# The first microseconds of a fused MLP kernel: x's first block turned by half-height products, its loads and the biases moved

## The chip, the cores and the metric

The kernel runs on one core of one Trainium2 chip. The metric is the device time of one execution in microseconds (us). Three runs of the kernel before gave a median of 265.3 us (264.82 to 265.36). TensorE is called PE here (its weight loads PEld), VectorE DVE, ScalarE ACT, GpSimd POOL, and SyncE, which only issues transfers, SP.

## The reference

The kernel computes a dense layer with a tanh-approximated GELU and a second dense layer, and all gradients, in bf16:

```python
B, S, D, F = 1, 2048, 448, 1792
h   = gelu(x @ w1 + b1)          # x: S x D, w1: D x F
out = h @ w2 + b2                # w2: F x D
# outputs: out, and from grad_out the gradients of x, w1, b1, w2, b2
```

## The kernel before, in words

The sequence is cut into four blocks of 512 rows. Within a block the 14 tiles of 128 columns of F are taken in seven pairs, so 28 pairs in all. For pair p, `u{p}` is x @ w1 (before GELU), `q{p}` is grad_out @ w2 turned; ACT and DVE make h and its derivative from u (steps `c`, `s`, `g`, `t` and `e`, `r`, `y`, `z`, `m`, `n`, `G`), and out and the gradient of x are summed from them on PE (`p`, `o`, `x`). After the four blocks, two stretches of full-height products (lines L781 and L835) make the gradients of w1 and w2.

Nothing is scheduled by a tool: four strings, `PE_ORDER`, `ACT_ORDER`, `DVE_ORDER` and `SP_ORDER`, list the steps of each engine in order, and each engine takes its own strictly in that order. The places of all buffers are fixed by name; the waits between engines follow from who reads and writes which buffer. A wait for a PSUM bank follows the tile: `bank0` to `bank5` are six tiles of one bank, but banks 6 and 7 are the two halves of one tile, `qb`.

In blocks 0 to 3 the contraction over D = 448 and over pairs is done by half-height products: the array's rows 0 to 63 and rows 64 to 127 hold different weights and write to two different banks at once (`run`, line L241). A run has a direction d = 1 or 2, in which the halves change banks; before the second direction a word from POOL's sequencer (line L236) tells PE that the first has ended.

The start, which the change touches:

- `xr01`, `xr12`, `xr24` load rows of x's first block (tiles of 128 rows: 0; 1; 2 and 3) into `TR`. `L0` to `L4` load w1's columns in five parts (into `w1f`), `Z0` to `Z2` the last rows of w1 for block 0 (into `gh_nat`), `K0` to `K3` load w2, `b1` and `b2` the biases. `X1`, `Y0`, `J..` and `I..` are loads that turn on the way.
- PE warms up with `W6` (six products of ones over 512 columns). `X0` to `X3` turn the four tiles of x by products with an identity matrix, which DVE makes at the start (`ident`, lines L560 to L569), four products of 128 columns each, full height, tile t into bank t. `w4` is four more products of ones, over 128 columns.
- The turned tiles are copied from PSUM into `xT`: X0 and X2 on DVE, X1 and X3 on ACT (line L583).
- Pair 0 of u is made in halves of 256 columns: `h0.1` and `h0.2` (the two directions, banks 4 and 5) need only X0 and X1; `h1.1` and `h1.2` (banks 2 and 3) need X2 and X3. Then `u1.1` and on.
- `B` spreads b2 over all partitions by a product with ones into bank 6, and `b2c` (L705, DVE) copies it to `b2_bc`. b1 is turned by four DVE transposes (`b1T`, L676); every evacuation of u (`c`, lines L411 on ACT and L413 on DVE) adds b1 from there.
- POOL clears three small tiles at the start, the buffer behind b2 among them (`b2z`, L672).

Of the kernel before, what the change touches and what calls it, by code (L numbers as in the profile page):

```python
# [127 lines left out]
SP_ORDER = """  # L128
xr01 xr24 b1 L1 Z1 L2 L3 K0 L4 K1 Z2 K2 K3 X1 R F Y0 J0 J1 J2 Y1 I0 E J3 I1 So0.1 So0.0 X2 H0 H1 H2 H3 H4 H5 H6 H7 H8 H9
T0 T1 H10 T2 H11 T3 H12 T4 H13 T5 So1.0 So1.1 T6 T7 H14 T8 Y2 H15 T9 X3 H16 T10 H17 Sx0.0 Sx0.1 T11 H18 H19 T12 H20  # L130
# [30 lines left out]
def make_plan(tc, ctx, x, w1, b1, w2, b2, grad_out, out_0, out_1, out_2, out_3, out_4, out_5):  # L161
    nc = tc.nc
    P = 128
# [63 lines left out]
    def run(slots, idle=False):  # L227


        first = slots[0]  # L230
        prev = [tail_of.get((first[i][0], 1 - i), (0, None, False)) for i in (0, 1)]
        prev = max([t for i, t in enumerate(prev) if t[2] or not first[i][4]], default=(0, None), key=lambda t: t[0])
        n_run[0] += 1
        word = None
        if prev[0] > seen[0]:
            word = nc.gpsimd.nop()  # L236
            tc.add_manual_dep(word.ins, prev[1].ins.name, DEP, reason="the run has ended")
            seen[0] = prev[0]
        for two in slots:
            for i, (b, n, l, r, st, sp) in enumerate(two):  # L240
                m = nc.tensor.matmul(bk_(b)[:, 0:n], lhsT=l, rhs=r, start=st, stop=sp, skip_group_check=True)  # L241
# [122 lines left out]
    def wake(n, w=SB):  # L364
# [3 lines left out]
        pe("wake", fn, [], [bank(("wake", len(pl.lists["PE"])), 7)], ("wake", n), (None, 0))  # L368

    def OP(p, i):  # L370
        c = p % NPB
        UN("o", p // NPB, 1 - i % 2, [2 * c, 2 * c + 1], 1 + i // 2)
# [16 lines left out]
    for p in range(NPAIR):  # L389
        val(("ub", p), F_UB[p])  # L390
        val(("h", p), ("hT", (p // NPB) % 2, p % NPB))
        val(("gh", p), ("ghT", (p // NPB) % 2, p % NPB))
        if p == NTR - 1:
            val(("xrows", 0), ("TR0", p))
            val(("xrows", 1), ("TR1", p))
# [85 lines left out]
    stage_of = {}  # L481
    val("b2z", ("stage", NST - 1))
    val("b2r", ("b2r",))
    val("ident", ("stage", 0))
# [68 lines left out]
    def LXN(t0, t1, eng="SP"):  # L553

        src = x2[t0 * P:t1 * P, :].rearrange("(t p) d -> p t d", p=P)
        dma(eng, f"xrows{t0}", x_rows[:, t0:t1, 0:D], src, [], [("xrows", t // 2) for t in range(t0, t1)], (t1 - t0) * 114688)

    def identity():
# [10 lines left out]
        nc.vector.tensor_scalar(out=ident, in0=nums128, scalar1=row, scalar2=None, op0=ALU.is_equal)  # L569

    def XT(t):

        def fn():
            for k in range(4):
                c = min(k * P, D - P)
                nc.tensor.matmul(bk_(t)[:, k * P:(k + 1) * P], lhsT=x_rows[:, t, c:c + P], rhs=ident,  # L576
                                 start=True, stop=True, skip_group_check=True)
        pe(f"xt{t}", fn, [("xrows", t // 2), "ident"], [bank(("xt", t), t)], ("s128", 4), (None, 0))

    def XC(t, eng):  # L580
        out = xT[0][:, :, EDGE + t * P:EDGE + (t + 1) * P]
        src = bk_(t)[:, :].rearrange("p (k s) -> p k s", k=4)
        fn = (lambda: nc.scalar.copy(out=out, in_=src)) if eng == "ACT" else (lambda: nc.vector.tensor_copy(out=out, in_=src))  # L583
        pl.op(eng, f"xc{t}", fn, [("xt", t)], [val(("xT", 0, t // 2), ("xT", 0, t // 2))], ("copy", 512))

# [58 lines left out]
    for t in PE_ORDER.split():  # L644
# [5 lines left out]
        elif k == "X":  # L650
            XT(int(a))
        elif k == "B":
            pe("b2u", lambda: nc.tensor.matmul(bk_(6)[:, 0:D], lhsT=one[0:64, 0:P], rhs=stage[NST - 1][0:64, 0, :], start=True, stop=True,  # L653
                                               skip_group_check=True), ["b2r", "b2z"], [bank(("b2u",), 6)], ("s448", 1), (None, 0))
        elif k == "d":
# [15 lines left out]
    pl.op("POOL", "b1z", lambda: nc.gpsimd.memset(b1n[:], 0.0), [], ["b1z"], ("tiny", 1))  # L671
    pl.op("POOL", "b2z", lambda: nc.gpsimd.memset(stage[NST - 1][0:64, 0, :], 0.0), [], ["b2z"], ("tiny", 1))  # L672

    def b1_turn():
        for i in range(4):
            nc.vector.transpose(out=b1T[32 * i:32 * i + 32, :], in_=b1n[:, 32 * i:32 * i + 32])  # L676

    step = {"g": G_, "s": S_, "t": T_, "e": E_, "r": R_, "y": Y_, "z": R2_, "m": M_, "n": N_, "G": GT_}
    for eng, order in (("ACT", ACT_ORDER), ("DVE", DVE_ORDER)):
        for t in order.split():  # L680
# [15 lines left out]
            elif k == "X":  # L696
                XC(int(a), eng)
            elif k == "D":
# [3 lines left out]
            elif t in ("b1", "b2"):  # L702
                (LB1 if t == "b1" else LB2)(eng)
            elif t == "b2c":
                pl.op(eng, "b2c", lambda: nc.vector.tensor_copy(out=b2_bc[:], in_=bk_(6)[:, 0:D]), [("b2u",)], ["b2"], ("evx", 1))  # L705
            elif t == "b1T":
                pl.op(eng, "b1T", b1_turn, ["b1n"], ["b1T"], ("tiny", 4))
# [171 lines left out]
```

## Time and profile before

| | before |
|---|---|
| median of three runs | 265.3 us (264.82 to 265.36) |
| the profiled execution's own time | 264.4 us |
| its span on the core | 262.6 us |
| PE busy, share of the span | 259.0 us, 99% |
| DVE, ACT busy | 200.5 us, 127.2 us |
| first product of u (`h0.1`) starts | 5.03 us |
| first product of `u2.1` starts | 8.36 us |

The span runs from the core's first instruction to its last; 1.8 us of the profiled time lie around it. In the rows of the timeline the first two numbers are start and length in us, then follow engine, line and operation, what it writes and reads, and in brackets the engine's idle time before it with what ended that. A matmul's length reaches to the modelled end of its pipeline, so products that follow each other overlap in the rows; their starts tell the pace.

### The profile page before, as it was taken

What the parts mean: (1) busy time and instruction counts of PE and PEld (TensorE: products, weight loads), DVE (VectorE), ACT (ScalarE), POOL (GpSimd) and SP (SyncE); (2) the same over time, 40 slices, a digit from 0 to 9 for tenths busy, and PEclk for the clock granted to TensorE, in tenths of its full rate; (3) what the DMA queues carried; (4) which work ended last, traced back from release to release, by engine and by line L of the source; (5) the groups of instructions that cost most, each with busy time, mean ns of one, the idle gap of its engine ahead of it and who ended that gap; (6) DMA issues with size and microseconds to landing.
All of it is one profiled execution on the core that took longest, in us unless ns stands there. A gap on an engine that the chain in (4) does not pass through costs nothing.

```text
span 262.6 us, 5353 instructions
## 1 busy us (share of the span) xinstructions
PE 259.0 (99%) x2185; PEld 148.3 (56%) x2185; DVE 200.5 (76%) x288; ACT 127.2 (48%) x163; POOL 14.6 (6%) x12
## 2 busy tenths in 40 slices
PE   8999999999999999999999999999999999999995
PEld 5444455555555566666666676765555555555554
DVE  6898398999999989999997995249999999310000
ACT  4899569836898956875896310011121111000001
POOL 1000000000000000000000000000000392400000
PEclk9999999999999999999999999999999999999999
DMA  7999979999999955882477933995799888987221
GB/s 200 296 245 186 208 157 215 273 297 200 279 178 217 244 136 44 190 207 40 109 203 245 226 42 75 270 196 107 143 230 160 157 200 179 171 194 185 70 72 35
DMA packets 120507, 46.50 MB, mean 177 GB/s; under 512 B 96687, under 2 KB 120353, under 8 KB 120482
## 3 DMA queue, kind: packets, MB, share of 16 engines
q1 hardware_dynamic: 119792, 45.71, 79.7%
q10 hardware_dynamic: 690, 0.44, 0.6%
q8 instruction: 17, 0.28, 0.5%
q14 instruction: 8, 0.07, 0.1%
HBM read 8.09 MB, written 14.28 MB: 85 GB/s over the span
## 4 chain that ended last, share of the span: by engine, by line
PE 99%; ACT 0%; issue 0%
PE bank L241 47%; PE qb L241 17%; PE bank L781 16%; PE bank L835 16%; PE qb L367 1%; PE bank L576 1%; ACT w_sb L840 0%; PE qb L653 0%
## 5 line engine op out<-in xcount | busy, mean ns | idle before, releaser
L241 PEld LDWEIGHTS <-HG 64*128 64x128 bf16 x896 | 54.9, 94 | 32.9 <-POOLq L236 1.9
L241 PE MATMUL qb<-gT,w2Tf 64*128 64x512 bf16 x392 | 52.8, 376 | 0.0
L241 PE MATMUL bank<-w_sb,HG 64*128 64x448 bf16 x448 | 48.3, 349 | 0.0
L241 PE MATMUL bank<-xT,w1f 64*128 64x512 bf16 (+1 forms) x360 | 47.5, 370 | 0.0
L241 PE MATMUL bank<-w1T_sb,HG 64*128 64x448 bf16 x448 | 47.2, 349 | 0.0
L476 DVE SCALAR_TENSOR_TENSOR HG<-TR,qb 128x1024 bf16<-128x1024 bf16 x28 | 34.1, 1217 | 12.6 <-PE qb L241 12.6
L835 PE MATMUL bank<-w2Tf,HG 128*128 128x448 bf16 (+2 forms) x240 | 42.6, 340 | 0.0
L781 PE MATMUL bank<-w1f,gh_nat 128*128 128x448 bf16 x224 | 42.5, 352 | 0.0
L835 PEld LDWEIGHTS <-HG 128*128 128x128 bf16 x240 | 22.9, 98 | 19.8
L781 PEld LDWEIGHTS <-gh_nat 128*128 128x128 bf16 x224 | 21.8, 98 | 20.6 <-issue 0.4
L241 PEld LDWEIGHTS <-w2Tf 64*128 64x128 bf16 x392 | 23.8, 94 | 16.9 <-POOLq L236 0.3
L461 ACT ACTIVATE TR<-TR 128x1024 bf16<-128x1024 bf16 x28 | 29.2, 1052 | 6.6 <-DVE TR L451 6.6
L241 PEld LDWEIGHTS <-w1f 64*128 64x128 bf16 x382 | 21.6, 94 | 17.8 <-POOLq L236 1.0
L804 DVE TENSOR_TENSOR w1T_sb<-w1T_sb,gh_nat 128x1792 f32<-128x1792 f32 x14 | 28.4, 2025 | 0.5
L786 ACT ACTIVATE TR<-bank 128x448 bf16<-128x448 f32 x14 | 7.6, 544 | 34.9 <-PE bank L781 34.9
L841 DVE CAST w_sb<-bank 128x448 bf16<-128x448 f32 x6 | 3.7, 623 | 25.9 <-PE bank L835 25.9
L840 ACT CAST w_sb<-bank 128x448 bf16<-128x448 f32 (+2 forms) x9 | 4.4, 491 | 37.7 <-PE bank L835 37.7
L810 POOL PARTITION_ALL_REDUCE w1T_sb<-w1T_sb x1 | 10.6, 10569 | 205.8 <-DVE w1T_sb L808 205.8
L436 ACT ACTIVATE TR<-gh_nat 128x1024 bf16<-128x1024 bf16 x15 | 15.7, 1052 | 11.5 <-DVE TR L471 11.5
L466 DVE TENSOR_SCALAR TR<-TR 128x2048 bf16<-128x2048 bf16 x28 | 19.1, 687 | 1.9 <-ACT TR L461 1.9
L456 DVE TENSOR_TENSOR TR<-TR,HG 128x1024 bf16<-128x1024 bf16 x28 | 19.1, 683 | 0.0
L471 DVE TENSOR_TENSOR TR<-TR 128x1024 bf16<-128x1024 bf16 x28 | 19.0, 685 | 0.1
(52 smaller groups left out, 191.2 us busy)
## 6 DMA issues: line engine op xcount, KB each, us to landing
hT_dram<-HG SPq DMA_DIRECT2D x28, 256.0 KB, 3.9
out_dram<-st SPq DMA_DIRECT2D x16, 224.0 KB, 2.4
w1f<-in_x_dram SPq DMA_DIRECT2D x2, 896.0 KB, 6.5
w2Tf<-in_grad_out_dram SPq DMA_DIRECT2D x2, 560.0 KB, 7.7
out_dram<-w_sb SPq DMA_DIRECT2D x2, 448.0 KB, 2.7
out_dram<-xT SPq DMA_DIRECT2D x2, 384.0 KB, 3.3
w_sb<-in_w_dram SPq DMA_DIRECT2D x1, 672.0 KB
w2Tf<-in_grad_out_dram SPq DMA_DIRECT2D x1, 672.0 KB
```

Of the source, the lines that this page charges most:

```text
L241: m = nc.tensor.matmul(bk_(b)[:, 0:n], lhsT=l, rhs=r, start=st, stop=sp, skip_group_check=True)
L436: pl.op("ACT", f"s{p}", lambda: nc.scalar.activation(out=TR[p % NTR][:, 1], in_=ubuf(p), func=ACT.Square, scale=sc), [("ub", p)], [v], ("a ...
L456: pl.op("DVE", f"R{p}", lambda: nc.vector.tensor_tensor(out=t[:, 1], in0=t[:, 1], in1=hblk(p), op=ALU.mult), [("r", p), ("h", p)], [val((" ...
L461: pl.op("ACT", f"t{p}", lambda: nc.scalar.activation(out=t[:, 0], in_=t[:, 0], func=ACT.Tanh), [("y", p)], [val(("t", p), ("TR0", p % NTR) ...
L466: pl.op("DVE", f"m{p}", lambda: nc.vector.tensor_scalar(out=t[:], in0=t[:], scalar1=1.0, scalar2=None, op0=ALU.subtract), [("t", p), ("r2" ...
L471: pl.op("DVE", f"n{p}", lambda: nc.vector.tensor_tensor(out=t[:, 0], in0=t[:, 0], in1=t[:, 1], op=ALU.mult), [("m0", p), ("m1", p)], [val( ...
L476: pl.op("DVE", f"G{p}", lambda: nc.vector.scalar_tensor_tensor(out=ghblk(p), in0=t[:, 0], scalar=2.0, in1=qb[:, :, :], op0=ALU.subtract, o ...
L781: nc.tensor.matmul(bk_(bk)[:, 0:D], lhsT=gh_nat[:, st // 4, ft, st % 4, :], rhs=x_nat[:, st, :], start=(st == 0), stop=(st == NS - 1))
L786: fn = (lambda dst=dst, src=src: nc.scalar.mul(out=dst, in_=src, mul=-0.5)) if eng == "ACT" else \
L804: nc.vector.tensor_tensor(out=hs3, in0=a, in1=gh_nat[:, st // 4, :, st % 4, :], op=ALU.add)
L810: pl.op("POOL", "gb1", lambda: nc.gpsimd.partition_all_reduce(gb1_w, hsum, channels=P, reduce_op=bass_isa.ReduceOp.add), ["hsc"], ["gb1"], ...
L835: nc.tensor.matmul(bk_(bk)[:, 0:d1 - d0], lhsT=h_nat[ft][:, st, :], rhs=g_nat[:, st, d0:d1], start=(st == 0), stop=(st == NS - 1))
```

## The change

The change rewrites the start, up to the first pair of u.

- X0 to X3 are turned by half-height products: rows 0 to 63 and 64 to 127 of a tile go through the two halves of the array into two banks (64 columns each, eight products a tile). X0 and X3 use banks 0 and 1, X1 banks 2 and 3, X2 banks 6 and 7. Every tile's two halves are copied on both engines, the first half on DVE, the second on ACT, 256 columns a copy.
- The warm-up is `W4`, and `f2`, `f5`, `f4` are new fillers: pairs of half-height products of ones over 128 columns, into banks 4 and 5. `h1.1` moves ahead of `B` and `h0.2`.
- All loads are issued by SP, the three of x first, then L0, Z0, b1; K1 moves ahead of L4. ACT issues none any more and starts with its table.
- b1 is turned by one product with the identity (16 columns, bank 6, still called `B`) and one DVE copy. b2 comes in by a load that repeats its row over 128 partitions (`b2`, behind R and F on SP); the product, the copy `b2c` and the clearing `b2z` are gone.

```diff
 PE_ORDER = """
-W6 X0 X1 w4 X2 X3 h0.1 B h0.2 h1.1 u1.1 h1.2 u1.2 u2.1 ...
+W4 f2 X0 X1 f5 X2 X3 f4 h0.1 h1.1 B h0.2 u1.1 h1.2 u1.2 u2.1 ...
...
 ACT_ORDER = """
-xr12 L0 Z0 b2 table X1 X3 c0A0 c0A1 s0 ...
+table X0.1 X1.1 X2.1 X3.1 c0A0 c0A1 s0 ...
...
 DVE_ORDER = """
-ident X0 X2 b1T c0B0 b2c c0B1 c1A c1B ...
+ident X0.0 X1.0 X2.0 X3.0 b1T c0B0 c0B1 c1A c1B ...
...
 SP_ORDER = """
-xr01 xr24 b1 L1 Z1 L2 L3 K0 L4 K1 Z2 K2 K3 X1 R F Y0 ...
+xr01 xr12 xr24 L0 Z0 b1 L1 Z1 L2 L3 K0 K1 L4 Z2 K2 K3 X1 R F b2 Y0 ...
...
+    def fill(n):
+        def fn():
+            run(n * [[(5 - i, P, one[64 * i:64 * i + 64, 0:P], one[64 * i:64 * i + 64, 0:P], True, True) for i in (0, 1)]], True)
...
+    X_BANKS = ((0, 1), (2, 3), (6, 7), (0, 1))
+
     def XT(t):
...
-                nc.tensor.matmul(bk_(t)[:, k * P:(k + 1) * P], lhsT=x_rows[:, t, c:c + P], rhs=ident,
-                                 start=True, stop=True, skip_group_check=True)
...
+                slots.append([(bks[i], (64 * k, 64), x_rows[64 * i:64 * i + 64, t, c:c + P],
+                               ident[64 * i:64 * i + 64, 64 * i:64 * i + 64], True, True) for i in (0, 1)])
+            run(slots)
...
-    def XC(t, eng):
-        out = xT[0][:, :, EDGE + t * P:EDGE + (t + 1) * P]
-        src = bk_(t)[:, :].rearrange("p (k s) -> p k s", k=4)
+    def XC(t, i, eng):
+        out = xT[0][:, :, EDGE + t * P + 64 * i:EDGE + t * P + 64 * i + 64]
+        src = bk_(X_BANKS[t][i])[:, 0:256].rearrange("p (k s) -> p k s", k=4)
...
-        dma(eng, "b2", stage[NST - 1][0:1, 0, :], b2.rearrange("(o d) -> o d", o=1), ["b2z"], ["b2r"], D * 2)
+        dma(eng, "b2", b2_bc[:], bass.AP(tensor=b2.tensor, offset=b2.offset, ap=[[0, P], [1, D]]), [], ["b2"], P * D * 2)
...
-            pe("b2u", lambda: nc.tensor.matmul(bk_(6)[:, 0:D], lhsT=one[0:64, 0:P], rhs=stage[NST - 1][0:64, 0, :], start=True, stop=True,
+            pe("b1u", lambda: nc.tensor.matmul(bk_(6)[:, 0:16], lhsT=b1n[0:64, :], rhs=ident[0:64, 0:16], start=True, stop=True,
...
-    pl.op("POOL", "b2z", lambda: nc.gpsimd.memset(stage[NST - 1][0:64, 0, :], 0.0), [], ["b2z"], ("tiny", 1))
...
-        for i in range(4):
-            nc.vector.transpose(out=b1T[32 * i:32 * i + 32, :], in_=b1n[:, 32 * i:32 * i + 32])
+        nc.vector.tensor_copy(out=b1T[:], in_=bk_(6)[:, 0:16])
```

On DVE, from the identity to the first evacuations of u, the rows before were these. A bracket names the engine or load whose semaphore the step waits for; `xT0` is the turned block, `ub0` the evacuated pair 0.

```order
L569 TENSOR_SCALAR st0_81<-st1_82 128x128 [waits DVE_49]
L583 CAST xT0_68<-bank0_89 128x4x128 [waits PE_49]
L583 CAST xT0_68<-bank2_91 128x4x128 [waits PE_49]
L676 STREAM_TRANSPOSE b1T_86<-b1n_85 32x32 [waits DMAHW5_49,Pool_49]
L676 STREAM_TRANSPOSE b1T_86<-b1n_85 32x32 x3
L413 TENSOR_SCALAR ub0_75<-bank5_94,b1T_86 128x256 [waits DVE_49,PE_49]
L705 CAST b2_bc_84<-qb_88 128x448
L413 TENSOR_SCALAR ub0_75<-bank3_92,b1T_86 128x256 [waits PE_49,Activation_49]
```

And these are the rows of the same place now.

```order
L573 TENSOR_SCALAR st0_81<-st1_82 128x128 [waits DVE_49]
L593 CAST xT0_68<-bank0_89 128x4x64 [waits PE_49]
L593 CAST xT0_68<-bank2_91 128x4x64 [waits PE_49]
L593 CAST xT0_68<-qb_88 128x4x64 [waits Activation_49]
L593 CAST xT0_68<-bank0_89 128x4x64 [waits PE_49]
L686 COPY b1T_86<-qb_88 128x16 [waits PE_49]
L419 TENSOR_SCALAR ub0_75<-bank5_94,b1T_86 128x256 [waits DVE_49,PE_49]
L419 TENSOR_SCALAR ub0_75<-bank3_92,b1T_86 128x256 [waits PE_49]
```

DVE has four half copies where it had two whole ones, one small copy for b1 where it had four transposes, and b2's copy is gone. The third half copy, X2's out of the tile `qb`, waits for ACT; the other three wait for PE.

On PE, before, these rows stand from the last weight load and product of `h0.1` (banks 5 and 4) over `B` to the start of `h0.2`.

```order
L241 LDWEIGHTS gh_nat_74
L241 MATMUL bank4_93<-xT0_68,gh_nat_74 128x256
L653 LDWEIGHTS const-bfloat16-1.0 [waits DMAHW6_49]
L653 MATMUL qb_88<-st2_83,const-bfloat16-1.0 128x448 [waits Pool_49]
L241 LDWEIGHTS w1f_64 [waits Pool_sequencer_49]
L241 MATMUL bank4_93<-xT0_68,w1f_64 128x256
```

Now the last product of `h0.1` is followed by `h1.1`.

```order
L242 LDWEIGHTS gh_nat_74
L242 MATMUL bank4_93<-xT0_68,gh_nat_74 128x256
L242 LDWEIGHTS w1f_64 [waits DVE_49]
L242 MATMUL bank3_92<-xT0_68,w1f_64 128x256 [waits Activation_49]
L242 LDWEIGHTS w1f_64
```

Further on, from the end of `h1.1`, the new `B` and the start of `h0.2` stand.

```order
L242 LDWEIGHTS gh_nat_74
L242 MATMUL bank2_91<-xT0_68,gh_nat_74 128x256
L665 LDWEIGHTS b1n_85 [waits DMAHW5_49,Pool_49]
L665 MATMUL qb_88<-st0_81,b1n_85 128x16
L242 LDWEIGHTS w1f_64 [waits Pool_sequencer_49]
L242 MATMUL bank4_93<-xT0_68,w1f_64 128x256
```

`h1.1`, which waits for the copies on DVE and ACT of X2 and X3, now stands between `h0.1` and `h0.2`, and the product over 448 columns is one over 16.

SP's first loads before, with two of x and L0 and Z0 on ACT's queue beside them:

```order
L517 DMA TR_80<-in_x_dram 128x448
L517 DMA TR_80<-in_x_dram 128x2x448
L517 DMA b1n<-in_b_dram 14x128 [waits Pool_49]
L517 DMA w1f<-in_w_dram 128x3x256
L517 DMA gh_nat<-in_w_dram 128x512 [waits DMAHW0_49]
L517 DMA w1f<-in_w_dram 128x3x256 [waits DMAHW1_49]
```

And now, with ACT's queue empty:

```order
L521 DMA TR_80<-in_x_dram 128x448 x2
L521 DMA TR_80<-in_x_dram 128x2x448
L521 DMA w1f<-in_w_dram 128x3x256
L521 DMA gh_nat<-in_w_dram 128x512
L521 DMA b1n<-in_b_dram 14x128 [waits Pool_49]
L521 DMA w1f<-in_w_dram 128x3x256
L521 DMA gh_nat<-in_w_dram 128x512
L521 DMA w1f<-in_w_dram 128x3x256 [waits DMAHW0_49]
```

Three issues that stood on ACT's queue (a tile of x, L0, Z0) now stand on SP ahead of b1 and L1.

More of the change, by code (lines that the diff above doesn't have):

```diff
@@ L210, in make_plan @@
     b2_bc = sb.tile([P, D], BF16, name="b2_bc")
-    b1n = sb.tile([32, P], BF16, name="b1n")
-    b1T = sb.tile([P, 32], BF16, name="b1T")
+    b1n = sb.tile([64, P], BF16, name="b1n")
+    b1T = sb.tile([P, 16], F32, name="b1T")
     tiny = sb.tile([P, 1], BF16, name="tiny")
@@ L368, in wake @@
         pe("wake", fn, [], [bank(("wake", len(pl.lists["PE"])), 7)], ("wake", n), (None, 0))
+    def fill(n):
+        def fn():
+            run(n * [[(5 - i, P, one[64 * i:64 * i + 64, 0:P], one[64 * i:64 * i + 64, 0:P], True, True) for i in (0, 1)]], True)
+        pe("fill", fn, [], [bank(("fill", len(pl.lists["PE"]), i), 4 + i) for i in (0, 1)], ("s128", n), ((4, 5), 1))
     def OP(p, i):
@@ L393, in make_plan @@
         if p == NTR - 1:
-            val(("xrows", 0), ("TR0", p))
-            val(("xrows", 1), ("TR1", p))
+            for i in range(4):
+                val(("xrows", i), ("xrows", i))
         for v in ("sq", "r", "r2", "m1"):
@@ L555, in LXN @@
         src = x2[t0 * P:t1 * P, :].rearrange("(t p) d -> p t d", p=P)
-        dma(eng, f"xrows{t0}", x_rows[:, t0:t1, 0:D], src, [], [("xrows", t // 2) for t in range(t0, t1)], (t1 - t0) * 114688)
+        dma(eng, f"xrows{t0}", x_rows[:, t0:t1, 0:D], src, [], [("xrows", t) for t in range(t0, t1)], (t1 - t0) * 114688)
     def identity():
@@ L651, in make_plan @@
             XT(int(a))
+        elif k == "f":
+            fill(int(a))
         elif k == "B":
[L653 to L654 removed]
+            pe("b1u", lambda: nc.tensor.matmul(bk_(6)[:, 0:16], lhsT=b1n[0:64, :], rhs=ident[0:64, 0:16], start=True, stop=True,
+                                               skip_group_check=True), ["b1n", "b1z", "ident"], [bank(("b1u",), 6)], ("s16", 1), (None, 0))
         elif k == "d":
@@ L703, in make_plan @@
                 (LB1 if t == "b1" else LB2)(eng)
-            elif t == "b2c":
-                pl.op(eng, "b2c", lambda: nc.vector.tensor_copy(out=b2_bc[:], in_=bk_(6)[:, 0:D]), [("b2u",)], ["b2"], ("evx", 1))
             elif t == "b1T":
-                pl.op(eng, "b1T", b1_turn, ["b1n"], ["b1T"], ("tiny", 4))
+                pl.op(eng, "b1T", b1_turn, [("b1u",)], ["b1T"], ("tiny", 4))
             elif t == "table":
```

21 lines of the change are left out of this document (11 added, 10 removed).

## The prediction

> **What bounds the kernel now.** I read the page first: busy time, then the chain that ended last.
>
> ```profile
> PE 259.0 (99%) x2185; PEld 148.3 (56%) x2185; DVE 200.5 (76%) x288; ACT 127.2 (48%) x163; POOL 14.6 (6%) x12
> ...
> PE 99%; ACT 0%; issue 0%
> ```
>
> PE is busy and on the chain for all but 1% of the span. A busy PE is not yet a PE at its pace, so the second view is the waits, for anything that PE or its weight loads waited for.
>
> ```profile
> PEld L241 <- POOLq L236: 3.2, 18, 0.3
> PEld L576 <- DMA TR<-in_x_dram: 0.7, 1, 0.7
> ```
>
> Weight loads waited 3.2 us for POOL's word in 18 places; they run ahead of the products, so most of that hides. No wait for a load, DVE or ACT stands in PE's stream after the start. So the end moves by as much as the start of the steady stream moves, nearly one for one, and work saved on DVE or ACT later on is worth nothing. The third view is therefore the timeline of PE at the start.
>
> ```profile
> 0.76 2.72 PE L367 MATMUL qb<-const-bfloat16-1.0 128*128 128x512 bf16 x6 [0.76 <-PEq L863]
> 3.34 1.01 PE L576 MATMUL bank<-st,TR 128*128 128x128 bf16 x8
> 4.15 0.45 PE L367 MATMUL qb<-const-bfloat16-1.0 128*128 128x128 bf16 x4
> 4.43 0.61 PE L576 MATMUL bank<-st,TR 128*128 128x128 bf16 x8
> 5.03 0.50 PE L241 MATMUL bank<-xT,w1f 64*128 64x256 bf16 x6
> ...
> 5.46 0.35 PE L653 MATMUL qb<-st,const-bfloat16-1.0 64*128 64x448 bf16 x1
> 5.75 0.50 PE L241 MATMUL bank<-xT,w1f 64*128 64x256 bf16 x5
> ...
> 6.09 0.49 PE L241 MATMUL bank<-xT,w1f 64*128 64x256 bf16 x6
> ...
> 6.53 0.81 PE L241 MATMUL bank<-xT,w1f 64*128 64x512 bf16 x6
> ...
> 8.36 0.81 PE L241 MATMUL qb<-xT,w1f 64*128 64x512 bf16 x6
> ```
>
> The reader sees W6, X0 and X1, w4, X2 and X3, then h0.1 (5.03), B (5.46), h0.2 (5.75), h1.1 (6.09), u1.1 (6.53) and, after h1.2 and u1.2, u2.1 (8.36). Two paces show. X0 and X1 took 4.15 − 3.34 = 0.81 us for eight products, about 0.10 us each; X2 and X3 start 0.055 us apart (4.43 plus eight of these is 4.87). The change to the fast pace lies within the 4.15 row, some 3.4 us after PE's first product.
>
> From h1.1 on the stream needs u2.1 − h1.1 = 8.36 − 6.09 = 2.27 us. After the change, B and h0.2 stand inside this stretch. h0.2 is 6.09 − 5.75 = 0.34; B, 16 columns in place of 448, I take at 0.05. So u2.1 will start 2.66 us after h1.1, and the break-even is h1.1 at 8.36 − 2.66 = 5.70 us. Later than that is lost time, earlier is gain. The question is when h1.1 starts.
>
> **The change part by part.** *When X0 can start.* Before, it was the identity that came last.
>
> ```profile
> 1.28 0.61 DVE L563 TENSOR_SCALAR st<-st 128x4 bf16<-128x4 bf16 x1
> ...
> 1.93 0.17 DVE L563 TENSOR_SCALAR st<-st 128x8 bf16<-128x8 bf16 x1
> ```
>
> ```profile
> 1.41 0.47 POOL L672 MEMSET st<- 64x448 bf16 x1
> ...
> 3.04 0.25 DVE L569 TENSOR_SCALAR st<-st 128x128 bf16<-128x128 bf16 x1
> 3.22 0.87 PEld L576 LDWEIGHTS <-TR 128*128 128x128 bf16 x8 [0.65 <-DMA TR<-in_x_dram]
> ```
>
> One tiny DVE step took 0.61 where its neighbour takes 0.17, and it ended at 1.89, with POOL's clearing for b2 (1.41 to 1.88). That clearing is removed, so the identity, done at 3.04 + 0.25 = 3.29, gains up to 0.44; clearing b1's tile still lies there, and I take 0.3, so 3.0. x's first tile was seen at 3.22 with two tiles in flight at once; alone in front of one queue it should be there by 3.0. X0 starts at 3.05 (bounds 2.9 and 3.34).
>
> *X0, X1 and f5.* Four steps of two half-height products each. No row shows 64-column products; the nearest are the 128-column ones, 0.10 slow and 0.055 fast. A step can't take less than nothing nor, two weight loads side by side, much more than one of these, so X0 and X1 take 0.43 each at the slow pace (bound 0.22): 3.05 to 3.91. f5's five steps, slow until 4.24 and then fast, end near 4.35.
>
> *X2 and the loads.* X2 waits for tiles 2 and 3.
>
> ```profile
> 0.72 0.87 SPq L517 DMA_DIRECT2D TR<-in_x_dram  x2
> ...
> 1.15 0.47 ACTq L517 DMA_DIRECT2D w1f<-in_w_dram  x1
> ...
> 1.65 0.54 ACTq L517 DMA_DIRECT2D gh_nat<-in_w_dram  x1
> ...
> 2.18 0.40 SPq L517 DMA_DIRECT2D w1f<-in_w_dram  x1
> ```
>
> ```profile
> TR<-in_x_dram SPq DMA_DIRECT2D x1, 224.0 KB, 3.1
> ...
> w1f<-in_w_dram ACTq DMA_DIRECT2D x1, 192.0 KB, 3.6
> gh_nat<-in_w_dram ACTq DMA_DIRECT2D x1, 128.0 KB, 3.6
> ```
>
> An issue on SP costs about 0.43 (two in 0.87). Tiles 2 and 3 become the third issue, at about 1.6 instead of 1.15; they landed 3.1 after issue with L0 sharing the engines beside them, which now queues behind. Bounds: 1.6 + 3.1 = 4.7 if the delay is all latency, 3.9 if only the bytes ahead count. I take up to 4.3, hidden behind f5: X2 runs 4.35 to 4.57, X3 to 4.8, f4 to 5.0, h0.1 at 5.0. L0 and Z0 are issued at about 2.1 and 2.5; before, at 1.15 and 1.65, they landed at 4.8 and 5.25. As shares of a full queue they land no later than before and cost nothing; with all their 3.6 us they land at 5.7 and 6.1, and h0.1's last step would wait until 6.1, h1.1 until about 6.2. L1 moves from 2.18 to 3.6 and, by its own 3.6, lands at 7.2, against u1.1 at about 6.9: 0 to 0.3.
>
> *The copies of X2 and X3, where I see the price.* h1.1 needs all four. The order shows that X2's copy on DVE waits for ACT, not for PE: both read the tile qb, so ACT's goes first and DVE's follows, and X3's DVE copy stands behind it. Their lengths come from whole copies and from the evacuations of u in both widths:
>
> ```profile
> 3.97 0.69 DVE L583 CAST xT<-bank 128x512 bf16<-128x512 f32 x1 [0.68 <-PE bank L576]
> ...
> 5.46 0.84 DVE L676 STREAM_TRANSPOSE b1T<-b1n 32x32 bf16<-32x32 bf16 x4
> ...
> 6.40 0.47 ACT L411 ACTIVATE ub<-bank,b1T 128x256 bf16<-128x256 f32 x1 [0.73 <-DVE b1T L676]
> 6.41 0.48 DVE L413 TENSOR_SCALAR ub<-bank,b1T 128x256 bf16<-128x256 f32 x1
> ...
> 11.29 0.74 DVE L413 TENSOR_SCALAR ub<-qb,b1T 128x512 bf16<-128x512 f32 x1
> ...
> 12.40 0.67 ACT L411 ACTIVATE ub<-qb,b1T 128x512 bf16<-128x512 f32 x1
> ```
>
> ```profile
> L583 ACT CAST xT<-bank x2: 586/586/586, 4.4 to 5.1; 128x512 bf16<-128x512 f32 x2
> ```
>
> Half the columns save 0.74 − 0.48 = 0.26 on DVE and 0.67 − 0.47 = 0.20 on ACT. A half copy is then 0.69 − 0.26 = 0.43 on DVE, and on ACT 0.59 − 0.20 = 0.39. The chain: X2's last product starts at 4.52 and is out about 0.2 later, 4.72 (a product of X3 at 4.82 still ended by 5.04: 4.43 + 0.61); ACT 4.76 to 5.15; DVE's X2 5.18 to 5.61; DVE's X3 to 6.04; then weight load and product: h1.1 at about 6.14. PE has only f4 and h0.1 (0.43) to run meanwhile and is idle from 5.45. Against 5.70 that is 0.44 us lost. Without the wait for ACT, DVE would finish at 5.65 and the change would break even.
>
> *What costs nothing.* h0.2's word is covered by h1.1, so the idle time at 5.75 goes; that is in the 5.70. b1's turn falls from 0.84 on DVE to one copy behind B; u's first evacuations start near 7.0, not 6.40, but the bank they free is next written by u3.1, over 2 us later. ACT's table moves into idle time. b2's load adds one issue of about 0.5 us on SP ahead of Y0 and the J loads.
>
> ```profile
> 20.67 5.60 SPq L529 DMA_TRANSPOSE w2Tf<-in_w_dram  x3
> ...
> 28.18 0.53 PEld L241 LDWEIGHTS <-w2Tf 64*128 64x128 bf16 x6
> ```
>
> The first of three J issues begins at 20.67 and is read at 28.18, so half a microsecond is hidden; if that cover were gone it would cost at most that half.
>
> *The clock.* PE's slow pace ended some 3.4 us after its first product, in a stream with nearly no hole. After the change W4 and f2 end at about 0.76 + 4 × 0.43 + 0.2 = 2.7, and PE is idle to 3.05, then works at half width in X0 and X1. If that holds back the fast pace, everything to the change runs at half pace; if not, nothing is lost. I take nothing, since 0.35 us in 3.4 is a tenth. The Trainium skill, "TensorE: Matmul & The Clock Gate", section "Why this matters for your kernels", asks to keep TensorE busy for at least 4 us continuously to reach the full clock; by the letter of that rule this change breaks the stretch, and the sum would be rival 1's. The trace before, with its 3.4 us, neither shows a hole nor what one does.
>
> *Sum.* 264.4 + 0.44 gives 264.85 us for a profiled execution. Its own time lies 0.9 under the median of the runs (265.3), and I add the same 0.45 there: **265.75 us**. Its own range: 265.35 (X2 in at 4.0, short copies: +0.05) to 266.15 (x or w1 land with their full latency: +0.85).
>
> **The rivals.** *1. The clock comes late.* Were the 3.4 us counted from 3.05, the fast pace begins at 6.5. Then X2 runs 4.5 to 4.9, X3 to 5.3, f4 to 5.75, h0.1 at 0.21 a step to 6.6, and h1.1 starts at 6.6: +0.9. A second such span would add at most half of 3.4, 1.7: +2.6. For it: a hole in the very stretch that warmed PE up. Against: it is short. 266.2 to 267.9 us, most likely 266.4.
>
> *2. The other side: the start moves ahead of the copies.* If 64-column steps take half the time, X0 ends at 3.2 and f5 near 4.0, X2's copies end near 5.5, and h0.1 goes as soon as L0 is in, as it did at 4.8. h1.1 can then follow at once at 4.8 + 0.05 + 0.43 = 5.28, if the copies are out: −0.43 at best. It decides where the copy chain ends before 5.70. Runs that keep the slow pace longer than the profiled one, as the 0.9 between it and the median may mean, also lose more in the old full-width start. Against it: the wait in qb. About −0.35, so 264.95 us.
>
> **How the numbers follow.** The forecast gets 0.55, rival 1 0.20, rival 2 0.25. About 0.2%, or 0.53 us, is what a measurement of this kernel can tell from no change. The forecast's range lies astride +0.53: 0.29 above, 0.26 within. Rival 1 is slower throughout. Of rival 2, 0.15 is faster (its best price is 0.43 and three runs spread by 0.5), 0.09 within, 0.01 slower. Together: slower 0.50, within 0.35, faster 0.15. The range takes in the forecast's own, rival 2 from 265.0, and rival 1 up to 267.0, and leaves out about 0.2.
>
> **What would show it.** Right: in the timeline after, X2's DVE copy starts where ACT's ends, h1.1 starts at 6.0 to 6.3 with PE's weight loads waiting for DVE (L593), and u2.1 at about 8.8. Products of h0.1 0.21 us apart beyond 5 us would show rival 1. h1.1 before 5.70 shows the forecast wrong on its main step, and a wait of PE for a load past 6 us shows that the loads and not the copies decide.

## The result, and the profile after

| | before | after |
|---|---|---|
| median of the runs | 265.1 us (264.43 to 265.83, 22 runs) | 266.02 us (264.87 to 266.88, 22 runs) |
| ratio after to before | | 1.0034, 95% interval 1.002 to 1.0049 |
| the profiled execution | 264.4 us, span 262.6 | 265.3 us, span 263.5 |
| `u2.1` starts | 8.36 us | 9.27 us |

The changed kernel is slower by 0.9 us at the median. Its times fall into two groups, with no run in the 0.57 us between them: 9 runs at 264.87 to 265.32 and 13 at 265.89 to 266.88; the profiled run is the slowest of the first group, and experiment 3 shows a run of the second.

The page of the kernel after, its busy times and its chain, has hardly moved:

```profile
PE 259.7 (99%) x2217; PEld 149.1 (57%) x2217; DVE 199.3 (76%) x286; ACT 127.4 (48%) x165; POOL 14.2 (5%) x11
...
PE 97%; DMA 1%; SPq 0%; ACT 0%; issue 0%
```

PE still carries the chain, but 1% of it is now a transfer, that of x. The waits of the kernel after, between 2 and 7.2 us (in total, times, longest), show who was late at the start:

```profile
PEld L242 <- DMA TR<-in_x_dram: 0.8, 3, 0.4
...
DVE xT L593 <- ACT xT L593: 1.1, 1, 1.1
...
PEld L242 <- DMA gh_nat<-in_w_dram: 0.5, 1, 0.5
```

Three waits for tiles of x, one for Z0 (`gh_nat`), and DVE's copy behind ACT's; PE itself never waits for a copy. The timeline of the kernel after gives their places:

```profile
1.63 0.43 SPq L521 DMA_DIRECT2D TR<-in_x_dram  x1
...
2.11 0.47 SPq L521 DMA_DIRECT2D w1f<-in_w_dram  x1
...
2.62 0.49 SPq L521 DMA_DIRECT2D gh_nat<-in_w_dram  x1
2.64 0.25 DVE L573 TENSOR_SCALAR st<-st 128x128 bf16<-128x128 bf16 x1
...
2.94 0.83 PE L242 MATMUL bank<-st,TR 64*128 64x64 bf16 x16
...
4.47 0.40 PE L242 MATMUL qb<-st,TR 64*128 64x64 bf16 x8 [0.17 <-DMA TR<-in_x_dram]
...
4.91 0.37 ACT L593 CAST xT<-qb 128x256 bf16<-128x256 f32 x1 [0.70 <-PE qb L242]
...
5.30 0.85 PE L242 MATMUL bank<-xT,w1f 64*128 64x256 bf16 x6
5.32 0.42 DVE L593 CAST xT<-qb 128x256 bf16<-128x256 f32 x1 [1.09 <-ACT xT L593]
...
5.66 0.41 DVE L593 CAST xT<-bank 128x256 bf16<-128x256 f32 x1
6.17 0.11 PEld L242 LDWEIGHTS <-gh_nat 64*128 64x128 bf16 x2 [0.51 <-DMA gh_nat<-in_w_dram]
6.18 0.40 PE L242 MATMUL bank<-xT,gh_nat 64*128 64x256 bf16 x2
...
6.37 0.79 PE L242 MATMUL bank<-xT,w1f 64*128 64x256 bf16 x6
...
9.27 0.62 PE L242 MATMUL qb<-xT,w1f 64*128 64x512 bf16 x4
```

Read the lengths of h0.1's six products: 0.85 us at 5.30, where before they took 0.50 at 5.03. PE still runs at its slow pace, and does so until about 7.0 (before: 4.3). Then Z0's weight load at 6.17 has waited 0.51 us. The copies end at 5.66 + 0.41 = 6.07, when PE isn't ready for them anyway.

In what follows one number stands for each profile: the start of `u2.1`. In all 14 profiled executions of this study the device time is that start plus 256.0 us (256.01 to 256.05: before 8.36 and 264.4, after 9.27 and 265.32, experiment 3 10.66 and 266.71), so everything that these kernels gain or lose lies ahead of `u2.1`.

### The profile page after: what moved, and what is told of

Same layout as the page of the kernel before. It is cut to its first block, busy times and chain, and to the rows that moved or that the text cites. A ratio compares the mean times of both kernels' runs of the same rounds, so it can differ in the third digit from the quotient of the medians.

```text
span 263.5 us, 5416 instructions
## 1 busy us (share of the span) xinstructions
PE 259.7 (99%) x2217; PEld 149.1 (57%) x2217; DVE 199.3 (76%) x286; ACT 127.4 (48%) x165; POOL 14.2 (5%) x11
## 4 chain that ended last, share of the span: by engine, by line
PE 97%; DMA 1%; SPq 0%; ACT 0%; issue 0%
PE bank L242 48%; PE qb L242 17%; PE bank L789 16%; PE bank L843 16%; DMA TR<-in_x_dram 1%; SPq L521 0%; ACT w_sb L848 0%; PE qb L665 0%
## 5 line engine op out<-in xcount | busy, mean ns | idle before, releaser
L242 PE MATMUL bank<-xT,w1f 64*128 64x512 bf16 (+1 forms) x360 | 48.2, 374 | 0.0
L242 PEld LDWEIGHTS <-w1f 64*128 64x128 bf16 x382 | 22.3, 95 | 16.9 <-POOLq L236 0.7
## 6 DMA issues: line engine op xcount, KB each, us to landing
hT_dram<-HG SPq DMA_DIRECT2D x28, 256.0 KB, 2.8
```

What stands on the lines that cost most here:

```text
L242: m = nc.tensor.matmul(bk_(b)[:, at:at + n], lhsT=l, rhs=r, start=st, stop=sp, skip_group_check=True)
```

## The experiments

The theory after the result had three parts, each with its own time: the *clock* (holes in PE's stream keep it at the slow pace; the word stands here for the pace that the starts of products show), the *loads* (Z0, issued fifth on SP, lands late), and the *copies* (the forecast's step: X2's two copies one after the other). Each part is a rival of the other two.

| run | median us (runs) | ratio to before, 95% | fastest run | runs over 265.8 | profiled: time, `u2.1`, fast pace from |
|---|---|---|---|---|---|
| before (four series) | 264.84 to 265.1 (127) | | 264.29 | 3 | 264.4, 8.36, 4.3 |
| after | 266.02 (22) | 1.002 to 1.0049 | 264.87 | 13 | 265.3, 9.27, 7.0 |
| 1 `e1_before_w4` | 265.77 (12) | 1.0025 to 1.0052 | 265.31 | 6 | 265.7, 9.65, 7.4 |
| 2 `e2_after_filled` | 265.05 (12) | 1.0001 to 1.0023 | 264.91 | 1 | 264.9, 8.89, 3.8 |
| 3 `e3_after_banks` | 265.41 (12) | 1.0011 to 1.0043 | 264.82 | 5 | 266.7, 10.66, 9.7 |
| 4 `e4_after_actloads` | 265.02 (12) | 0.9992 to 1.0011 | 264.58 | 0 | 265.1, 9.02, 6.7 |
| 5 `e5_filled_actloads` | 265.02 (11) | 1.0001 to 1.0019 | 264.82 | 0 | 265.1, 9.05, 5.8 |
| 6 `e6_and_banks` | 264.67 (12) | 0.9982 to 1.0001 | 264.37 | 0 | 264.4, 8.35, 4.5 |
| 7 `e7_and_order` | 264.76 (11) | 0.9986 to 1.0004 | 264.49 | 0 | 265.1, 9.09, 5.5 |
| 8 `e8_before_bias` | 264.76 (12) | 0.9982 to 1.0003 | 264.38 | 0 | 264.5, 8.52, 4.0 |
| 9 `e9_first_hole` | 265.02 (11) | 0.9995 to 1.0012 | 264.92 | 0 | 265.0, 9.00, 4.6 |
| 10 `e10_second_hole` | 265.16 (11) | 0.9988 to 1.0032 | 264.92 | 1 | 265.1, 9.08, 5.7 |
| 11 `e11_bias_order` | 264.76 (12) | 0.998 to 1.0003 | 264.38 | 0 | 265.1, 9.06, 6.6 |
| 12 `e12_before_sploads` | 265.23 (11) | 1.0 to 1.0019 | 265.01 | 0 | 265.3, 9.32, 5.2 |

The last column's point is read from the starts of single products: it is the start of the first product that the next one follows in about half the earlier time (in run 9 a hole of 0.24 us lies just ahead of it). 1 to 4, 5 to 8 and 9 to 12 each shared a chip and a series of the kernel before (medians 264.84, 264.95 and 265.07).

**1. A hole in the kernel before.**

```diff
-W6 X0 X1 w4 X2 X3 h0.1 ...
+W4 X0 X1 w4 X2 X3 h0.1 ...
```

> The kernel before with one thing changed: W4 in place of W6, so that PE stands idle for about 0.9 us (2.4 to 3.3 us) before X0, which itself cannot move, since the identity is done at 3.29. Clock theory (a hole in PE's start holds back its fast pace): the median rises by 0.4 to 1.0 us against the kernel before and the runs spread over more than 1.5 us, and where the profiled run is a late one, products of h0.1 and h1.1 start 0.21 us apart and not 0.107. Copy theory (the copies of X2 and X3, with DVE's behind ACT's, set the end) and load theory (the late landing of Z0 and of x's tiles 2 and 3 sets it): neither is touched here, so no change within 0.15 us.

Ratio 1.0039: 0.93 us at the median, from nothing but 0.94 us of idle PE ahead of X0. PE's timeline in this kernel:

```profile
0.76 1.86 PE L367 MATMUL qb<-const-bfloat16-1.0 128*128 128x512 bf16 x4 [0.76 <-PEq L863]
3.36 1.03 PE L576 MATMUL bank<-st,TR 128*128 128x128 bf16 x8 [0.73 <-DMA TR<-in_x_dram]
...
5.60 0.82 PE L241 MATMUL bank<-xT,w1f 64*128 64x256 bf16 x6
```

The last of the four products starts at 1.99 and takes 0.43, so PE is free at 2.42 and X0 starts at 3.36 (the row's 0.73 counts from the modelled end of the pipeline; holes are counted from the starts of products here and below). X0 starts where it did before (3.34), so the hole takes no time itself. But X0 to X3 and h0.1 all run slowly (0.82 for the six products of h0.1), and h0.1 begins 0.57 later. One execution proves little here (run 11 has a late one without a hole); the 12 runs do: their fastest, 265.31, lies above 29 of the 35 runs of before beside them (264.29 to 265.4). So the clock as a cause is shown, in the kernel before, by itself.

**2. The changed kernel with its holes filled.**

```diff
-W4 f2 X0 X1 f5 X2 X3 f4 h0.1 ...
+W4 f4 X0 f2 X1 f8 X2 X3 f4 h0.1 ...
```

> The changed kernel with its holes in PE's stream filled: f4 for f2 before X0, a new f2 between X0 and X1, f8 for f5 ahead of X2. Nothing else moves. Clock theory: the fast pace comes at 4.2 to 5 us in nearly all runs, the spread falls to that of the kernel before (about 1 us), the median falls by 0.5 to 0.9 us against the changed kernel (266.0), to 265.1 to 265.5. Then h1.1 is held at about 6.2 us by the copies and by Z0. Copy theory and load theory: the fillers stand in waits that stay, so no gain: 266.0, within 0.2.

Ratio 1.0012 where the change has 1.0034. The fast pace is back, and the next wait shows:

```profile
5.12 0.50 PE L242 MATMUL bank<-xT,w1f 64*128 64x256 bf16 x6
6.11 0.28 PE L242 MATMUL bank<-xT,gh_nat 64*128 64x256 bf16 x2 [0.49 <-DMA gh_nat<-in_w_dram]
```

h0.1's first products take 0.50 again, and its last step waits for Z0 to 6.11. What the faster pace won before that point is waited away. The fillers, too, ran faster and ended before x landed, so a hole ahead of X2 (4.14 to 4.51) is still there; it came behind the fast pace.

**3. Other banks alone.**

```diff
-    X_BANKS = ((0, 1), (2, 3), (6, 7), (0, 1))
+    X_BANKS = ((0, 1), (6, 7), (2, 3), (0, 1))
```

> The changed kernel with X1 in banks 6 and 7 and X2 in banks 2 and 3, so that X1's two copies, not X2's, are taken one after the other. Copy theory: DVE's copies of X2 and X3 end some 0.3 to 0.4 us earlier (near 5.7 in place of 6.07), and the median falls by 0.3 to 0.4 us against 266.0. Clock theory and load theory: h1.1 stands behind h0.1, which the slow pace and Z0 (6.13) hold until 6.37, so the end moves by less than 0.1 us; in runs with an early clock only Z0 holds it.

X2's copies now run side by side and DVE is done at 5.59 in place of 6.07, yet the ratio, 1.0027 (1.0011 to 1.0043), can't be told from the change's own. Its profile is of a run of the upper group:

```profile
5.23 0.85 PE L242 MATMUL bank<-xT,w1f 64*128 64x256 bf16 x6
...
7.79 1.70 PE L242 MATMUL bank<-xT,w1f 64*128 64x256 bf16 x7
...
10.66 0.60 PE L242 MATMUL qb<-xT,w1f 64*128 64x512 bf16 x4
```

Its products stay slow until 9.7 us, and that is what this run of the upper group is: 266.71 us with the start of `u2.1` 2.3 us later than before. No gain from copies that end sooner shows while PE is slow and Z0 late.

**4. ACT's loads given back.**

```diff
 ACT_ORDER
-table X0.1 ...
+xr12 L0 Z0 table X0.1 ...
 SP_ORDER
-xr01 xr12 xr24 L0 Z0 b1 ...
+xr01 xr24 b1 ...
```

> The changed kernel with the loads of x's second tile, L0 and Z0 issued by ACT again, ahead of its table, as before; all else as changed. Load theory: Z0 lands near 5.3 in place of 6.13, x's tiles 2 and 3 near 4.2 in place of 4.43, h0.1 is not broken and the median falls by 0.25 to 0.5 us against 266.0. Copy theory: the chain of copies starts 0.2 us earlier with X2 and the median falls by 0.2 at most. Clock theory: the hole before X2 shrinks by 0.2 us and the wait inside h0.1 goes, so part of the late runs turn early: 0.2 to 0.6 us less, and a spread still near 2 us.

Ratio 1.0002 (0.9992 to 1.0011): the loss is gone, though the holes stay and the profiled run is slow until 6.7.

```profile
5.31 0.85 PE L242 MATMUL bank<-xT,w1f 64*128 64x256 bf16 x6
5.95 0.42 PE L242 MATMUL bank<-xT,gh_nat 64*128 64x256 bf16 x2
6.16 0.74 PE L242 MATMUL bank<-xT,w1f 64*128 64x256 bf16 x6
```

Z0's step follows h0.1 at 5.95 without a wait; Z0 had landed at 5.50. None of 12 runs is in an upper group. So the three loads cost time, and they also bear on the clock: more than its theory had expected, which had part of the late runs turn early and a spread still near 2 us (it is 0.8).

**5. Both repaired.** As 4, with

```diff
-W4 f2 X0 X1 f5 X2 X3 f4 h0.1 h1.1 B h0.2 ...
+W5 f4 X0 X1 f8 X2 X3 f4 h0.1 h1.1 B h0.2 ...
```

> The changed kernel with its two first costs taken away together: the stretch of PE before X2 is filled without holes (W5, f4 ahead of X0, f8 ahead of X2), and tile 1 of x, L0 and Z0 are issued by ACT again. Left over from the change are the half-height turn, the half copies with X2's pair one after the other, and the biases. Theory of the copies as the cost that is left: DVE's X3 copy ends near 6.0 to 6.1, h1.1 starts at about 6.15 with PE's weight loads waiting for DVE, u2.1 at about 8.8, and the time is 0.3 to 0.45 us over the kernel before, about 265.2. Theory that clock and loads were all of it: h0.1 at about 5.1 in steps of 0.107, h1.1 follows it without a wait, and the time is at or under the kernel before, 264.8 or less. A late clock again would show as steps of 0.21 us in h0.1 and some 0.9 us more.

Ratio 1.001 (1.0001 to 1.0019). PE's row for h1.1 and DVE's for the copies:

```profile
6.43 0.50 PE L242 MATMUL bank<-xT,w1f 64*128 64x256 bf16 x6 [0.17 <-DVE xT L593]
```

```profile
5.62 0.42 DVE L593 CAST xT<-qb 128x256 bf16<-128x256 f32 x1 [1.02 <-ACT xT L593]
5.96 0.41 DVE L593 CAST xT<-bank 128x256 bf16<-128x256 f32 x1
```

Here at last PE waits for DVE, which waited for ACT: the forecast's step, once what covered it is gone. But filling the holes on top of run 4 shows no gain: both medians are 265.02, and run 4, with the same copies, has the faster fastest run (264.58 against 264.82). Fillers have a price too: at the slow pace f8 ends at 4.67, where run 4's f5 ended at 4.23, and X2 stands behind it even where x has landed (here x came later still, at 4.73).

**6. And the banks.** 5 with the banks of 3.

> As the run with holes filled and ACT's loads, but X1 and X2 change banks: X1 uses the two halves of the tile qb and X2 banks 2 and 3, so that X2's two copies run side by side and it is X1's that follow each other, earlier. Theory of the copies: the copies end at about 5.55 in place of 6.05, h1.1 starts at about 5.65 to 5.75, and the time falls by about 0.3 us against that run, to within 0.15 of the kernel before. Theory that the copies cost nothing: no change against that run (within 0.1).

264.67, 0.35 under run 5, as the theory of the copies wanted; the two intervals just touch (0.9982 to 1.0001 against 1.0001 to 1.0019). The PE rows, and DVE's last two copies:

```profile
5.06 0.49 PE L242 MATMUL bank<-xT,w1f 64*128 64x256 bf16 x6
5.62 0.28 PE L242 MATMUL bank<-xT,gh_nat 64*128 64x256 bf16 x2
5.74 0.49 PE L242 MATMUL bank<-xT,w1f 64*128 64x256 bf16 x6
...
8.35 0.83 PE L242 MATMUL qb<-xT,w1f 64*128 64x512 bf16 x6
```

```profile
4.91 0.76 DVE L593 CAST xT<-bank 128x256 bf16<-128x256 f32 x2
```

h1.1 starts at 5.74 behind Z0's step and the copies' end (5.67) at once. Not all of the 0.69 between the two profiles' h1.1 is the copies': in run 5's execution tiles 2 and 3 happened to land at 4.73, here at 4.30 (X2 then stood behind the fillers until 4.59). With its three costs repaired the change stands at `u2.1` = 8.35 against 8.36: no gain that shows.

**7. Order of h0.2 and h1.1.** 6 with `X2 X3 h0.1 B h0.2 h1.1` in place of `X2 X3 f4 h0.1 h1.1 B h0.2`.

> As the run with the banks changed, but h0.1, B and h0.2 stand ahead of h1.1 again, as in the kernel before, and the filler f4 behind X3 is gone. Theory: h0.1 starts as L0 lands, about 4.9, h0.2 at about 5.5, and they fill the time in which the copies end; h1.1 starts at about 5.8, u1.1 at 6.25, u2.1 at about 8.1 in place of 8.36, and the kernel is 0.2 to 0.3 us faster than the one before, about 264.6. If the load of Z0 (landing at about 5.4 to 5.5) or the word ahead of h0.2 holds PE instead, it is the same as before within 0.1 us.

264.76 against 264.95, ratio 0.9986 to 1.0004: the same as before, and not better than 6. The profiled execution is the slowest of its 11, since tiles 2 and 3 landed 4.1 us after their issue (X2 at 5.33); h0.2 at 6.47 stood 0.27 behind B. Inconclusive on the order itself.

**8. The biases alone, in the kernel before.**

```diff
 ACT_ORDER
-xr12 L0 Z0 b2 table ...
+xr12 L0 Z0 table ...
 SP_ORDER
-... R F Y0 ...
+... R F b2 Y0 ...
```

with `B`, b1's copy and b2's load as in the change.

> The kernel before with nothing of the change but the biases: b1 turned by one product of 16 columns and one DVE copy, b2 by a load that repeats its row, POOL's clearing for b2 and the copy of b2 gone. Loads, warm-up, the turn of x and its copies stay as they were. Theory: B falls from 0.29 us (5.46 to 5.75) to about 0.05 to 0.15, of which the word ahead of h0.2, no longer covered, takes part; W6 still ends at about 3.3, so that an earlier identity is worth nothing; the time is 0.1 to 0.25 us under the kernel before. If the word for h0.2 eats all of it, or the repeated load of b2 delays a later load that is waited for, no change or slower.

Ratio 0.9993 (0.9982 to 1.0003): no difference shown. The rows of PE and of its weight loads say why:

```profile
5.63 0.17 PE L651 MATMUL qb<-st,b1n 64*128 64x16 bf16 x1
...
5.91 0.22 PEld L241 LDWEIGHTS <-w1f 64*128 64x128 bf16 x5 [0.23 <-POOLq L236]
5.91 0.50 PE L241 MATMUL bank<-xT,w1f 64*128 64x256 bf16 x5
```

B to h0.2 is 0.28 us, as it was with 448 columns (5.46 to 5.75): POOL's word ahead of h0.2 takes what B gives back.

**9. The first hole filled alone.**

```diff
-W4 f2 X0 X1 f5 X2 X3 ...
+W5 f4 X0 X1 f5 X2 X3 ...
```

> The changed kernel with only its first hole of PE filled: W5 in place of W4, f4 in place of f2 ahead of X0; the second hole, before X2 (4.09 to 4.48), stays, and so do the loads on SP and the copies. Theory that the first hole, at 2.6 to 3.4, is what keeps the pace slow: the fast pace comes near 4.3, the time falls by the 0.5 to 0.7 us that filling both holes brought, to 0.1 to 0.15% over the kernel before. Theory that a hole at any place starts the count again: the pace stays slow until 7 or later and the time is 0.3% over the kernel before, as with both holes. Copies (6.0) and Z0 (6.1) would in any case keep h1.1 from starting before 6.1.

X0 then starts at 3.38 with X1 right behind it, so the hole between the two is gone as well. Ratio 1.0003 (0.9995 to 1.0012), none of 11 runs over 265.5, as the theory of the first hole had it, or better. The row of Z0's step is what is left, and the fastest run (264.92) is half a microsecond over the fastest of before:

```profile
6.28 0.28 PE L242 MATMUL bank<-xT,gh_nat 64*128 64x256 bf16 x2 [0.64 <-DMA gh_nat<-in_w_dram]
```

This wait is itself a hole of 0.8 us, counted by starts. It came behind the fast pace and did not bring the slow one back: h1.1's products, from 6.40 on, stand 0.11 apart.

**10. The second hole filled alone.**

```diff
-W4 f2 X0 X1 f5 X2 X3 ...
+W4 f2 X0 X1 f9 X2 X3 ...
```

> The changed kernel with only its second hole filled (f9 in place of f5 ahead of X2); W4 and f2 leave PE idle from about 2.64 to X0 as before. Theory that the first hole alone delays the fast pace: as the changed kernel, slow until 6.5 to 7 or later, 0.3% over the kernel before. Theory that the second hole is what starts the count again: fast pace by about 6.3 in every run, and the upper group of times (0.9 us above the lower) goes away; the time is 0.1 to 0.2% over the kernel before.

One of 11 runs at 266.58, the others 264.92 to 265.39; fast from 5.7 in the profiled one. Taken alone this is what the theory of the second hole wanted, as run 9 is what that of the first wanted. Together they leave neither: whichever of the two holes is filled, the upper group goes away, or nearly. The changed kernel itself was not run in the series of these two; its upper group is known from its own 22 runs and from run 3 (5 of 12).

**11. The biases and h1.1 ahead, in the kernel before.** 8 with `h0.1 h1.1 B h0.2`.

> The kernel before with the biases' part of the change and the order h0.1, h1.1, B, h0.2, nothing else: full-height turn of x, W6, and loads as before. With the biases alone, h0.2 took up the time that B gave back, since it waited for POOL's word until 0.28 us behind B's start; here h1.1 covers the word. The copies of X2 and X3 (whole, on two engines) end near 5.45, when h0.1 ends. Theory: h1.1 at about 5.6, h0.2 at about 6.15 behind B without a wait, u2.1 at about 8.2 to 8.25, and the kernel is 0.15 to 0.3 us faster than the one before (264.65 to 264.8 where that has 264.95). If Z0's landing (5.4 to 5.5) or the longer copies hold h1.1 to 5.7 or later, the same within 0.1 us. The end of every profiled run so far lies 256.0 us behind the start of u2.1, so that start tells the time.

264.76 against 265.07, ratio 0.998 to 1.0003: not shown to be faster. The profiled execution missed the expectation for a reason of its own; its rows of X2, X3 and h0.1:

```profile
4.59 1.06 PE L574 MATMUL bank<-st,TR 128*128 128x128 bf16 x8
5.58 0.82 PE L241 MATMUL bank<-xT,w1f 64*128 64x256 bf16 x6
```

The warm-up and the turn are those of the kernel before, without a hole, and still this execution is slow until 6.6, with 265.1 us. So a late clock comes without a hole too, and the spread of the kernel before (nearly all of its runs lie between 264.3 and 265.8) may hold such executions.

**12. The loads alone, in the kernel before.**

```diff
 ACT_ORDER
-xr12 L0 Z0 b2 table ...
+b2 table ...
 SP_ORDER
-xr01 xr24 b1 ...
+xr01 xr12 xr24 L0 Z0 b1 ...
```

> The kernel before with only the loads' part of the change: tile 1 of x, L0 and Z0 are issued by SP, behind tile 0 and around tiles 2 and 3, in place of ACT; K1 and L4 as before, everything else too. Theory of the loads: tile 1 lands 0.4 later or is seen with the identity at 3.3 anyway; tiles 2 and 3 land at about 4.45 (X2 started at 4.43, no loss), L0 at about 5.05 (h0.1 stood at 5.03, no loss), Z0 at 6.1 in place of 5.3: h0.1's last step waits for it until about 6.1 in place of 5.4, h0.2 and h1.1 follow, and the time is 0.5 to 0.65 us over the kernel before. Theory that the loads cost nothing, as the forecast had it: within 0.1 us of it.

The profile is the expected one:

```profile
5.42 0.50 PE L241 MATMUL bank<-xT,w1f 64*128 64x256 bf16 x6
6.31 0.28 PE L241 MATMUL bank<-xT,gh_nat 64*128 64x256 bf16 x2 [0.39 <-DMA gh_nat<-in_w_dram]
```

h0.1's last step waits for Z0 until 6.31 (before: 5.35). The ratio is smaller than expected, 1.001 (1.0 to 1.0019), and the spread says why: all 11 runs lie between 265.01 and 265.39. The fastest is 0.6 over the fastest of before in its series (264.43), as the theory of the loads wanted; the slowest, 265.39, is no slower than slow runs of before (265.55 among others). This would follow if executions with a late clock lose nothing more, since PE waits for Z0 in any case; that is argued from the spread, not shown.

The fastest runs nearly sort by this alone. With Z0 on SP (after, 2, 3, 9, 10, 12) they are 264.82 to 265.01; with Z0 on ACT (before, 4, 6, 7, 8, 11) 264.29 to 264.58. Two runs with Z0 on ACT stand outside: run 5, held by the copies in its profile, with 264.82, and run 1, with its hole, with 265.31.

## Why the prediction was right in its number and wrong in its main step

The forecast was 265.75 us, 0.45 over the 265.3 that three runs of before gave; measured were 266.02 and 0.92 over 265.1, the median of 22. The number lies in the range and within the forecast's own 265.35 to 266.15, but the added time is twice the forecast's, and is the price that rival 1 gave (0.9; its 266.2 to 267.9 us, counted from the same 265.3, begin above the measured time). That the time still came out near is in part luck: a base 0.2 too high made up for part of a price 0.47 too low, and the price came from other steps than the forecast's.

- *The end moves with u2.1's start, one for one*: right, to 0.02 us in 14 executions. Nothing behind it changed; the loads, J and b2 among them, stayed covered.
- *X0 at 3.05*: 2.94. The identity gained 0.40 (from 3.29 to 2.89) where 0.3 was taken: POOL's clearing was the cause, and DVE's slowed step is gone: run 8, without the clearing and with the loads of before, has the identity at 2.88, and run 12, with it, at 3.30. It bought nothing, since PE then waited for tile 1 (X1 at 3.37).
- *X0, X1 0.43 each*: 64-column steps stand 0.05 us apart at the slow pace, half of what was taken (the bound of 0.22 was the value). Again nothing was bought: X2 stood at 4.47 for its load, 0.12 later than the 4.35 of the forecast.
- *X2's DVE copy waits for ACT, copies 0.39 and 0.43, the chain to 6.04*: right in mechanism and in every size (0.37, 0.42, end at 6.07). Wrong was that it sets the end: PE was not ready for h1.1 at 6.1. Run 3 took the chain away without a gain that shows; only where clock and loads were repaired (5 against 6, intervals that touch) was it worth about 0.35, near the forecast's 0.44.
- *The clock taken at nothing, "since 0.35 us in 3.4 is a tenth"*: this is the step that failed. Four holes of 0.2 us or more came, not one (0.20 and 0.22 around X0, 0.38 ahead of X2, 0.24 at Z0; behind W4 stands a smaller one of 0.14). Run 1 prices one of 0.94 us at 0.93, and run 9, with the first two filled, takes the ratio from 1.0034 to 1.0003. The trace of before could show neither, as the prediction said; the mistake was to value what no row showed at its good end.
- *L0 and Z0 "land no later than before and cost nothing"*: wrong for Z0, the other failed term. Issued 0.97 us later (2.62 against 1.65), it landed at 6.13 in place of 5.27. The bound given for it (6.1, "h0.1's last step would wait until 6.1, h1.1 until about 6.2") is what happened. L0 bore the forecast out more nearly: issued 0.96 later, it landed at 5.02 in place of 4.79. So a landing does not simply move with its issue. These are the two loads in the answer for the kernel after (KB, us from issue to landing), where before both took 3.6:

```profile
w1f<-in_w_dram SPq DMA_DIRECT2D x1, 192.0 KB, 2.9
...
gh_nat<-in_w_dram SPq DMA_DIRECT2D x1, 128.0 KB, 3.5
```

- *Z0 in all profiles*: with Z0 on SP it landed at 6.07 to 6.31 (six profiles), with Z0 on ACT at 5.27 to 6.03 (eight).
- The sum over the profile: h1.1 at 6.37 in place of 6.14 (Z0 and h0.1's slow pace) is 0.23, and 2.90 from there to `u2.1` in place of 2.66 (h1.1 itself still slow: 0.74 for what took 0.44) is 0.24. With the forecast's 0.44 these make the 0.91 of the two profiles.
- *Rival 2*, the start ahead of the copies, needed h0.1 at 4.8 and Z0 in time. Neither came.
- The marks named beforehand: X2's DVE copy did start where ACT's ends; h0.1's products 0.21 apart beyond 5 us and PE's wait for a load past 6 us came both, so by the prediction's own test rival 1 and the loads decided, not the copies.

The Trainium skill, "TensorE: Matmul & The Clock Gate", section "Why this matters for your kernels", spoke against the change: at least 4 us of unbroken work to reach the full clock. Run 1 agrees, and so does run 4's profiled execution, slow until 6.7 with holes of 0.55 and 0.25 us in this stretch. It is not the whole of it: the ratio of run 4 to before shows no loss, run 11 was as late without a hole, and before and run 8 were fast 3.5 and 3.2 us after their first product.

What stays open: which sum of holes, in which stretch, puts an execution into the upper group. Filling the first hole (and with it the one between X0 and X1), or the one ahead of X2, or giving ACT its three loads back, each removes the upper group nearly or wholly (0 of 11, 1 of 11, 0 of 12, against 13 of 22). No run varied one hole's length by steps, so why each of them is enough is not shown. Nor is it shown how the 0.92 divides: what one repair gains depends on which others are made.

## What to carry to other kernels

At the start of this kernel a hole in TensorE's stream cost nothing where it lay and up to a microsecond later, through the pace of everything until the fast pace came. Such a hole can be filled with products of ones that end as the next load lands; fillers that end later hold up the work behind them. Judge by many runs, since one execution shows only one of the cases. When loads are gathered on one queue, count each issue (0.4 to 0.5 us here) and ask for the last load that is waited for: its landing moved by nearly as much as its issue here. Several late things at the same point hide one another: the gain of one repair shows only when the others are made, so price each alone and all together.

## What the runs showed of the hardware that was not expected

- *The point of the change to the fast pace differs widely between executions with the same start.* Before and runs 8, 12 and 11 have the same PE order up to X3 and no hole of 0.1 us or more up to there: 4.3, 4.0, 5.2 and 6.6 us. The Trainium skill, "TensorE: Matmul & The Clock Gate", section "What's actually happening", tells of a free-running window of about 3.4 us, so that the point varies by 500 ns either way from run to run. The traces agree that it varies, but over 2.6 us, and the measurement decides.
- *The profile's clock column does not show it.* In this row of the windows of the kernel before (length; PE, PEld, DVE, ACT, POOL busy; clock; DMA share; GB/s) the clock stands at 1.00 for a stretch in which nearly all products took twice their later time:

```profile
0.50:4.20 3.70, 3.44 (x15) 1.68 (x16) 2.38 (x10) 1.41 (x2) 0.97 (x6) 1.00 0.67 186
```

- *The same load, issued at the same time, landed 3.1, 3.6 and 4.1 us later* (tiles 2 and 3 of x in the profiled executions of runs 6, 5 and 7), a difference as large as the effects under study.
- *A 16-column product in place of 448 columns gained nothing* where the next run of products waits for a word from another engine: 0.28 us from B to h0.2 in run 8 against 0.29.
